# Stores on GpSimd's and SyncE's queues, states cast from those carried on, a plain copy as last step: lightning attention and an MLP on one core

## The chip, the cores and the metric

One core of a Trainium2 chip. The metric is the device time of one execution in microseconds, the median of several runs. A profile of one further execution gives the rows that are quoted.

## What is computed

Causal linear attention with a decay `lam` per head, over 4 batches, 8 heads, 768 positions and head width 64, and behind it a two-layer MLP with SiLU on the 3072 rows of 512. Cut to what matters:

```python
# attention, block of 64 positions at a time; kv_state starts at zero
intra = (qb @ kb.T * lam ** (i - j) for i >= j) @ vb
inter = (qb * lam ** (i + 1)) @ kv_state
out[:, :, sl] = intra + inter
kv_state = lam ** 64 * kv_state + (kb * lam ** (63 - i)).T @ vb
# MLP
h = x @ w_in                       # 3072 x 512 @ 512 x 2048
out = (h / (1 + exp(-h))) @ w_out  # 3072 x 2048 @ 2048 x 512
```

Inputs and output are float32; the kernel multiplies in bfloat16 and sums in float32.

## The kernel before

The sequence is cut into 12 pairs of blocks, 256 positions each, three pairs to a batch; the MLP counts in row blocks of 128. Each pair n is loaded (k, q, v, one DMA each on SyncE's queue), cast to bfloat16 (`cast`), its v scaled by the decay (`scale`, tile `vd`), and k and q are transposed: by TensorE for the first four pairs, by a DMA on SyncE's queue after them. From pair 3 on, all small TensorE products of a pair stand in one **burst** (`burst(n)`): the state of pair n (L639), the scores of pair n (L650), and the output of pair n-1 (L613, L606), on 64x64 quarters of the array. VectorE then masks the scores (`mask`, tile `st`), adds the carried state (`y`, L768), and from `y` makes two things: `xe`, the state in bfloat16 that the output products read (tiles `xs_all`, `xe_all`), and `xf`, the float32 state carried on; both are products of `y` and `lam_be` (`mult`, L394; `xe` on VectorE, `xf` mostly on GpSimd). `xt` evacuates the attention output.

The MLP's **first product** is `product1` (tag `first`, L916) with SiLU on ScalarE (`silu`, L933); its **second product** is `product2` (tag `second`, L955), evacuated by `result` and stored by `stored`. For the rows of groups 7 and 8 (row blocks 16 to 23) the first product, and for row blocks 12 to 23 the second product, are made from seven half-size products in place of eight (`product1_of_four`, L1214; `product2_of_four`, tag `seven`, L1096). They need sums of quarters: of the weights (`b`, `w`), of the inputs (`x`), and of the hidden values (`a`, tile `asum`). In groups 12 and 16 most sums `a` are made by DMA: a copy on SyncE's queue, then an accumulating DMA on GpSimd's queue (L1083). Results already summed in one PSUM bank are copied to another (`to P`, `to B`, `to R`, and `to u` in the first product), where TensorE goes on adding. Such a bank must have been filled by matmuls before; `fills` and `seeded` only assert it.

What runs when is set by `Planner`: every piece of work is a task with a key, the engines it may run on with assumed costs, its dependencies and its buffers. `order` plays the plan through once, at build time; each engine's instruction order is fixed by it, and nothing is decided on the chip. `SHIFT` moves the keys of single tasks, `HOME` fixes an engine for some. PSUM has 8 banks; a burst takes up to 7 at a time. A dummy product of `ones` (L1282) fills TensorE's gaps in the first 17 us.

At the end stand the seven products of the last four row blocks (20 to 23). The last, `m6`, is made for one row block after the other (`split`); each half is then finished by VectorE, which subtracts `o21` from the bank, and stored by ScalarE's queue:

```python
for u in range(2):
    o = Buf("rawh")
    c22 = add(at(7), {"DVE": 0.42}, lambda e, u=u, o=o: sum_of(e, osb_of(o, 1)[:, 0], part(R, u), o21.tile[:, u], AL.subtract), ...)
    stored((at(7.3)[0], 7), halves_of[1], slice(128 * us[2 + u], 128 * us[2 + u] + 128), o, c22)
```

All 25 output stores are issued by ScalarE. Line numbers are those of the kernel before; in the changed one `mult` is L411, `copy` L404 to L408, `sum_of` L1014, `stored` L961, the first product L932, the second L974 and L1123, the accumulating DMA L1110.

Of the kernel before, what the change touches and what calls it, by code (L numbers as in the profile page):

```python
# [25 lines left out]
class Buf:  # L26

    __slots__ = ("pool", "slot", "left", "tile", "pe")

    def __init__(self, pool):  # L30
        self.pool, self.slot, self.left, self.tile, self.pe = pool, None, 0, None, 0

# [5 lines left out]
def family(tag):  # L38

    return tag[:2] if isinstance(tag, tuple) and len(tag) > 2 else "none"  # L40


class Planner:
# [8 lines left out]
    SHIFT = {('a', 12, 1, 0): 11.25, ('a', 12, 2, 1): 1.25, ('a', 12, 6, 0): 4.25, ('cast', 11, 1, 1): -6.75, ('cast', 4): -10,  # L52
             ('cast', 5, 0, 1): 1.25, ('cast', 6): 5.75, ('cast', 7): 0.25, ('cast', 9, 0, 0): 3, ('cast o', 0, 0): 1.75,
             ('cast o', 0, 3): 7, ('cast o', 1, 1): 0.25, ('cast o', 2, 0): 3, ('first', 2, 2): 0.5, ('first', 2, 6): -7,
             ('first', 3): -6.5, ('first', 5, 3): -10, ('first', 5, 5): -10.75, ('first', 6, 12): 9, ('first', 6, 14): 9.5,
             ('first', 6, 8): 1.5, ('first', 7, 1, 1): -0.75, ('first', 7, 1, 2): 2.5, ('first', 7, 1, 4): 5, ('first', 7, 2, 7): 4,
             ('first', 8, 1, 1): -9.25, ('first', 8, 1, 7): 5.25, ('first', 8, 2, 1): 6, ('first', 8, 2, 2): -9.25,
             ('first', 8, 3, 1): -10.75, ('first', 8, 3, 5): 5.25, ('load w', 3, 1): -1.5, ('m3', 12): 0.5, ('mask', 5): 3,
             ('mask', 6, 1, 0): 5, ('mask', 7, 0, 0): 4, ('mask', 8, 1, 0): 1.25, ('result', 2): -6, ('result', 7): 10,
             ('scale', 11): 8.75, ('scale', 3, 0): -1, ('scale', 5, 0): -9, ('scale', 6, 0): 11.75, ('scale', 8, 0): 4,  # L60
             ('score', 1): 3, ('second', 0): -11.25, ('second', 11): 9.75, ('second', 5): 0.5, ('seven', 12): 2.25,
             ('seven', 12, 1): -0.5, ('seven', 12, 7): -6.25, ('seven', 16): 3.5, ('seven', 16, 2): 1.75, ('seven', 16, 3): -10.75,
             ('seven', 16, 4): -2.75, ('seven', 16, 6): 2.25, ('seven', 20): 3.5, ('seven', 20, 3): -1.5, ('seven', 20, 6): 0.75,
             ('seven', 20, 7): 0.5, ('silu', 3): -7.25, ('silu', 3, 4): 7, ('silu', 7): 7.75, ('silu', 8): 10, ('states', 2): 12,
             ('turn', 1): -1, ('turned', 0, 0, 1): 2.5, ('turned', 0, 1, 0): 5.5, ('turned', 1): -3.25, ('turned', 2, 0, 1): -1,
             ('w', 1): 6.5, ('w', 3): 1.25, ('x', 7): 2, ('x', 7, 3): 8.75, ('xe', 0, 0, 1): 4.5, ('xe', 3, 0, 0): 1.5,
             ('xe', 6, 0, 0): -9.5, ('xf', 9): 2.75, ('xt', 4): -2, ('xt', 8): 10.25, ('xt', 9, 1): 8.75, ('y', 10): 10,
             ('y', 11, 0, 0): -4.25, ('y', 5): 1.75}
    HOME = {('cast', 11, 1, 0): 'ACT', ('cast', 11, 1, 1): 'ACT', ('cast', 3, 0, 1): 'ACT', ('cast', 4, 0, 0): 'DVE',
            ('cast', 5, 0, 1): 'ACT', ('cast', 9, 0, 0): 'DVE', ('cast o', 0, 3): 'POOL', ('cast o', 1, 1): 'DVE',  # L70
            ('cast o', 2, 0): 'ACT', ('cast o', 2, 1): 'ACT', ('cast o', 2, 2): 'POOL', ('cast w', 1, 3): 'POOL',
            ('m3', 12): 'DVE', ('result', 2): 'DVE', ('to B', 16): 'ACT', ('to u', 8, 1): 'DVE', ('turned', 0, 0, 1): 'DVE',
            ('turned', 0, 1, 0): 'ACT', ('turned', 2, 0, 1): 'DVE', ('u3', 8, 2): 'ACT', ('w', 4, 0): 'POOL', ('w', 4, 1): 'POOL'}
# [8 lines left out]
    def add(self, key, on, fn, deps=(), bufs=(), nbytes=0, kind=None, prior=(), late=0.0, tag=None, lock=False):  # L82
        key = key if isinstance(key, tuple) else (key,)
        key = (key[0] + (self.SHIFT.get(tag, 0.0) + self.SHIFT.get(family(tag), 0.0)),) + key[1:]
        if tag in self.HOME:
            on = {self.HOME[tag]: on[self.HOME[tag]]}
        t = Task(key, on, fn, deps, list(bufs), nbytes, kind, prior, late)
        t.tag, t.lock = tag, lock
        for b in t.bufs:
            b.left += 1  # L90
            b.pe += "PE" in t.on
        self.tasks.append(t)
        return t

    def order(self):
# [11 lines left out]
        started = set()  # L107
# [58 lines left out]
        while len(out) < len(self.tasks):  # L166
# [8 lines left out]
            while release and release[0][0] <= now:  # L175
                _, _, b = heapq.heappop(release)
                self.pools[b.pool].append(b.slot)
                last[b.pool].discard(id(b))
                if not last[b.pool] and b.pool in self.becomes:
                    to, slots = self.becomes[b.pool]  # L180
                    self.pools[to] += slots
            for e in free:
# [8 lines left out]
                while ready[e]:  # L191
# [7 lines left out]
                    if any(len(self.pools[p]) < n for p, n in need.items()):  # L199
# [26 lines left out]
                for b in t.bufs:  # L226
                    if b.slot is None:
                        b.slot = self.pools[b.pool].pop(0)
# [38 lines left out]
def kernel(  # L267
# [10 lines left out]
    nc = tc.nc  # L278
# [18 lines left out]
    LOADED, MOVED, HEAD = (4, 9), (12, 16), (1.8, 1.8, 1.2, 0.6)  # L297
    TKEY, SEVENS, LAG, WSKEY, FIRST_SEVENS = 9.0, 12, 5.0, 14.0, (16, 20)
# [207 lines left out]
    def prepare(n):  # L506
# [32 lines left out]
        for g, ms in enumerate(parts):  # L539
            w = len(ms) / 4  # L540
            if n in CROSSED:
                ck.append([add((s - 1.0, g, i, c), {"DVE": 0.7 + 0.16 * c, "ACT": 1.07 + 0.17 * c}, lambda e, i=i, c=c: cross(e, i, c),
# [5 lines left out]
            cv.append(add((s - 0.8, g), {"POOL": 0.15 + 2.15 * w} if n in AWAY else {"DVE": 0.12 + 1.15 * w}, lambda e, g=g: scale_v(e, g), deps=[loads[2, g]],  # L548
# [34 lines left out]
    def burst(n, alone=False):  # L583
# [5 lines left out]
        if o:  # L589
            ob = [Buf("bank") for _ in range(2)]  # L590
# [35 lines left out]
        if new:  # L626
            kq, kqT, vd, ck, cv, turned, kq_of, t_of = ready_of[n]
            final = n % NB == NB - 1
            db, sb_ = Buf("bank"), [[Buf("bank") for _ in halves] for _ in range(2)]
# [47 lines left out]
        while rows[0] or rows[1]:  # L677
# [5 lines left out]
                max([i + 1 for i, (what, k, _, _) in enumerate(order) if what == "s" and k < 2], default=0), len(order)]  # L683
        ts, prev, spent = [], 0, -cost
# [24 lines left out]
    def attention(n):  # L709
# [41 lines left out]
        for g, ms in enumerate(parts):  # L751
# [5 lines left out]
            for c in range(len(xes)):  # L757
# [6 lines left out]
                if old:  # L764
                    src = ys[c]

                    def new_y(e, src=src, old=old, d_of=d_of, sl=sl):
# [9 lines left out]
                made[c] += [add((s + late - 0.9, 2, g), {"POOL": 0.1 + 0.6 * w} if (n, c) in XAWAY else {"DVE": 0.15 + 0.27 * w},  # L777
                                lambda e, b=b, so=so, j=j, d=d, sl=sl, x=crossed: mult(e, xe_of(b)[halves[d == halves[0]] if x else d, sl, j], so()[d],
                                                                                               rate[d, sl]),
                                deps=sd, bufs=[src, b], tag=("xe", n, g, c), lock=n >= PORT and bool(old)) for d, j in ways]  # L780
                if not final:
# [3 lines left out]
                            deps=sd, bufs=[src, f], tag=("xf", n, g, c), lock=n >= PORT and bool(old))  # L785
                    old = f, [t]
# [106 lines left out]
    full = set()  # L893

    def fills(b):

        full.add(PSUM[b.pool] + b.slot)

    def seeded(b):
        assert PSUM[b.pool] + b.slot in full  # L900

    def product1(gi):
# [6 lines left out]
        for mg in range(KO // per):  # L909
            bank, g, one = Buf("bank"), gq[mg // 4], Buf("one")  # L910
            base = us[0] - us[0] % 4 + mg * per / 4

            def mm(e, j, ko, bank=bank, mg=mg):
# [4 lines left out]
                fills(bank)  # L918
# [23 lines left out]
    def stored(key, cs, rows, osb, done):  # L942

        def store(e):
            nc.scalar.dma_start(out=out[rows, cs].rearrange("(u p) c -> p u c", p=128), in_=osb.tile)

        add(key, {"ACT": 0.1}, store, deps=[done], bufs=[osb], nbytes=(rows.stop - rows.start) * (cs.stop - cs.start) * 4e-6,
            kind=LARGE)

    def product2(u):  # L950
        gi, gp = group_of[u]
        bank, two, osb = Buf("bank"), Buf("two"), Buf("osb")

        def mm(e, ko):
            nc.tensor.matmul(psum_of(bank), lhsT=gs[gi, ko][1](1, 128 * gp, 128)[:, 0], rhs=w_out_bf[:, ko],  # L955
                             start=(ko == 0), stop=(ko == KO - 1))
            fills(bank)
# [31 lines left out]
    def duplicate(key, src, dst, deps, tag, sign=1):  # L989
        def go(e):  # L990
            seeded(dst)
# [23 lines left out]
    def sums_of_w_out():  # L1015
        for i, m in enumerate(SEVEN):
# [6 lines left out]
            def build(e, h, b=b, qs=qs, op=op):  # L1023
# [3 lines left out]
            ts = [add((TKEY + i / 4, h), {"DVE": 0.7}, lambda e, h=h, build=build: build(e, h),  # L1027
                      deps=[wload["o", 8 * r + 4 * h + ko] for r in range(2) for ko in range(4)], bufs=[b], tag=("b", m, h), lock=True,
                      prior=loaded[0])
                  for h in range(2)]  # L1030
            bsum[m] = b, [ts[ko // 4] for ko in range(8)], lambda ko, b=b: b.tile[:, ko]

    def product2_of_four(us):
        s = LAG + us[0]
        final = us[-1] == NU - 1
        A, P, B = [Buf("bank") for _ in range(3)]
        copies = {}

        R = [Buf("bank") for _ in range(2 if final else 1)]
# [9 lines left out]
        def product(i, m, bank, opens, after=(), split=False):  # L1049
# [8 lines left out]
            else:  # L1058
                for h in range(2):
# [10 lines left out]
                    if not moved:  # L1070
                        ts = add((key - 1.2, 8, h), {"DVE": 0.7}, lambda e, t=sum_tile, x=x, y=y: sum_of(e, t(), x(4), y(4), AL.subtract if m == 1 else AL.add),
# [18 lines left out]
            for p in ([(0,), (1,)] if split else [(0, 1)]):  # L1090
                for ko in range(8):
                    buf, ready, lhs = left[ko]

                    def mm(e, p=p, ko=ko, lhs=lhs):
# [3 lines left out]
                        fills(bank[0])  # L1098
# [23 lines left out]
        m5 = product(2, 5, [A], False, after=[d3, k3])  # L1122
        c12 = add(at(3), either, lambda e: copy(e, osb_of(o12), two_of(A)), deps=m5, bufs=[A, o12], tag=("c12", tag))  # L1123
        stored((at(3.3)[0], 7), halves_of[1], top, o12, c12)
        m1 = product(3, 1, [P], False, after=[d4])
        m2 = product(4, 2, [B], False, after=[d4])
# [220 lines left out]
```

## Time and profile before

| | |
|---|---|
| median of 3 runs | 205.26 us (204.59 to 206.97) |
| the profiled execution: its own time | 204.97 us |
| its span, first to last instruction | 203.1 us |
| granted TensorE clock | 1.000 |
| busy TensorE (PE), VectorE (DVE), ScalarE (ACT), GpSimd (POOL) | 196.7, 148.0, 130.5, 45.0 us |
| moved by DMA | 44.44 MB |

The profile is of one execution. A row of an engine gives the start and the length of an instruction; a wait is put down to what came last. A matmul's length is longer than the distance to the next one, since matmuls overlap; where TensorE's pace is meant, the distance of starts counts. DMA-issuing instructions of ScalarE and SyncE are not counted as busy, GpSimd's are.

### The profile page before, as it was taken

To read this page: it belongs to the slowest core of one execution; us is meant where nothing else is said; L and a number is where in the kernel's file an instruction comes from. 1 tells how busy PE (TensorE), PEld (TensorE's weight loads), DVE (VectorE), ACT (ScalarE), POOL (GpSimd) and SP (SyncE) were. 2 spreads that over 40 slices of the span, in tenths; PEclk is the share of its full clock that TensorE was granted. 3 is DMA by queue.
4 is the path that set the end of the run, shared out by engine and by line. 5 is a ranking of instruction groups with operands and counts; after the bars stand their busy time and mean duration, and the time that the engine had idled before them with its cause. 6 is when DMAs were issued, how large, how long until landed. Compare 5 with 4: busy or idle time off the path is not lost.

```text
span 203.1 us, 6063 instructions
## 1 busy us (share of the span) xinstructions
PE 196.7 (97%) x2585; PEld 144.7 (71%) x2585; DVE 148.0 (73%) x248; ACT 130.5 (64%) x199; POOL 45.0 (22%) x58
## 2 busy tenths in 40 slices
PE   7999999999999999999999999999999999999993
PEld 2677887767775557657775455558888888888882
DVE  3797859497995929569796978889585463667762
ACT  3697878568892675635887896363768696737400
POOL 4105320323100320002020045049803306000000
PEclk9999999999999999999999999999999999999999
DMA  4999999999999999999997415049995988311133
GB/s 104 329 372 383 368 360 277 367 314 375 267 259 304 247 338 302 183 307 272 307 240 223 103 58 133 28 147 233 175 125 159 219 239 151 65 52 52 61 119 135
DMA packets 71723, 44.44 MB, mean 219 GB/s; under 512 B 18448, under 2 KB 64528, under 8 KB 71696
## 3 DMA queue, kind: packets, MB, share of 16 engines
q1 hardware_dynamic: 61168, 33.56, 58.6%
q0 software_dynamic: 5376, 4.20, 14.1%
q10 hardware_dynamic: 5152, 6.30, 8.5%
q8 instruction: 20, 0.33, 0.6%
q14 instruction: 7, 0.06, 0.1%
HBM read 27.27 MB, written 6.29 MB: 165 GB/s over the span
## 4 chain that ended last, share of the span: by engine, by line
PE 89%; DMA 4%; DVE 3%; ACT 1%; issue 1%; POOL 0%
PE banks L916 25%; PE banks L955 21%; PE banks L1096 18%; PE banks L1214 12%; DMA raw_w<-in_moe_w_out_dram 4%; PE banks L1282 4%; PE banks L606 3%; PE banks L650 2%; PE banks L613 1%; DVE st L394 1%; PE banks L639 1%; PE banks L558 1%; DVE vd L394 1%; PE banks L820 1%; DVE xt L394 1%
## 5 line engine op out<-in xcount | busy, mean ns | idle before, releaser
L916 PE MATMUL banks<-xt,w_in_bf 128*128 128x256 bf16 (+1 forms) x448 | 64.6, 288 | 0.2 <-POOL w_in_bf L391 0.2
L933 ACT ACTIVATE g<-banks 128x512 bf16<-128x512 f32 x64 | 46.2, 743 | 25.3 <-PE banks L916 22.2
L916 PEld LDWEIGHTS <-w_in_bf 128*128 128x128 bf16 x448 | 43.0, 98 | 15.2 <-POOL w_in_bf L391 0.3
L955 PE MATMUL banks<-w_out_bf,g 128*128 128x512 bf16 x192 | 48.5, 379 | 0.3 <-POOL w_out_bf L391 0.3
L394 DVE TENSOR_TENSOR st<-banks,tri 128x512 bf16<-128x512 f32 (+1 forms) x42 | 30.0, 757 | 4.3 <-PE banks L650 3.6
L387 ACT ACTIVATE kq<-raw 64x512 bf16<-64x512 f32 (+3 forms) x41 | 29.7, 756 | 3.7 <-DMA raw<-in_k_dram 1.0
L955 PEld LDWEIGHTS <-g 128*128 128x128 bf16 x192 | 18.2, 98 | 18.4
L394 POOL TENSOR_TENSOR xf<-y,lam_be 128x256 f32<-128x256 f32 (+1 forms) x13 | 11.5, 888 | 65.1 <-DVE y L768 65.1
L394 DVE TENSOR_TENSOR xt<-banks,lam_xe 128x512 bf16<-128x512 f32 x24 | 16.0, 684 | 10.1 <-PE banks L606 10.1
L1096 PE MATMUL banks<-bsum,g 128*128 128x256 bf16 x160 | 21.6, 273 | 0.0
L1096 PEld LDWEIGHTS <-asum 128*128 128x128 bf16 x176 | 17.2, 98 | 2.0
L1083 POOL DMA_DIRECT2D asum<-g x8 | 13.3, 1834 | 19.0 <-PE banks L1214 11.4
L1096 PEld LDWEIGHTS <-g 128*128 128x128 bf16 x160 | 15.6, 98 | 1.9
L394 DVE TENSOR_TENSOR vd<-raw,lam_v 128x1024 bf16<-128x1024 f32 (+1 forms) x13 | 15.5, 1190 | 1.4 <-DMA raw<-in_v_dram 0.7
L1214 PE MATMUL banks<-xsum,wsum 128*128 128x256 bf16 x96 | 14.4, 273 | 0.0
L1231 ACT ACTIVATE g<-tmp 128x512 bf16<-128x512 f32 x16 | 12.1, 773 | 3.2 <-DVE tmp L997 3.0
L1083 POOL DMA_DIRECT2D g<-g x8 | 14.1, 2520 | 0.0
L1214 PEld LDWEIGHTS <-wsum 128*128 128x128 bf16 x128 | 12.4, 98 | 1.5
L1231 ACT ACTIVATE g<-banks 128x512 bf16<-128x512 f32 x16 | 11.7, 739 | 2.4 <-PE banks L1214 2.3
L1096 PE MATMUL banks<-w_out_bf,asum 128*128 128x256 bf16 x96 | 13.1, 273 | 0.0
L997 DVE TENSOR_TENSOR tmp<-banks,tmp 128x512 f32<-128x512 f32 x16 | 10.9, 685 | 2.3 <-PE banks L1214 1.3
L389 DVE CAST kq<-raw 64x1024 bf16<-64x1024 f32 (+3 forms) x17 | 9.6, 577 | 3.5 <-DMA raw<-in_k_dram 2.6
(83 smaller groups left out, 251.3 us busy)
## 6 DMA issues: line engine op xcount, KB each, us to landing
out_dram<-osb ACTq DMA_DIRECT2D x23, 256.0 KB, 2.8
raw<-in_k_dram SPq DMA_DIRECT2D x11, 512.0 KB, 6.3
raw<-in_q_dram SPq DMA_DIRECT2D x11, 512.0 KB, 6.8
raw<-in_v_dram SPq DMA_DIRECT2D x11, 512.0 KB, 6.9
raw_w<-in_moe_w_in_dram SPq DMA_DIRECT2D x8, 512.0 KB, 7.7
raw_w<-in_moe_w_out_dram SPq DMA_DIRECT2D x8, 512.0 KB, 7.5
asum<-g SPq DMA_DIRECT2D x8, 256.0 KB, 2.6
asum<-g POOLq DMA_DIRECT2D x8, 256.0 KB, 5.4
```

The lines of the kernel that those rows point to most:

```text
L387: nc.scalar.activation(o, i, AF.Copy)
L389: nc.vector.tensor_copy(o, i)
L394: (nc.vector if e == "DVE" else nc.gpsimd).tensor_tensor(o, a, b, op=AL.mult)
L916: nc.tensor.matmul(t[:, j, :], lhsT=w_in_bf[:, ko, 128 * m:128 * m + 128], rhs=xt[gi].tile[:, ko, :], start=(ko == 0), stop=(ko == KI - 1))
L933: nc.scalar.activation(t.rearrange("p j (c a r) -> p (j c) r a", c=n // U, r=2), psum_of(bank).rearrange("p (jc r a) -> p jc r a", r=2, a= ...
L955: nc.tensor.matmul(psum_of(bank), lhsT=gs[gi, ko][1](1, 128 * gp, 128)[:, 0], rhs=w_out_bf[:, ko], start=(ko == 0), stop=(ko == KO - 1))
L997: (nc.vector if e == "DVE" else nc.gpsimd).tensor_tensor(o, x, y, op=op)
L1083: nc.gpsimd.dma_start(out=x(4) if here else t(), in_=y(4), accum_op=AL.add)
L1096: nc.tensor.matmul(part(bank, u), lhsT=lhs(u), rhs=b_of(ko), stop=ko == 7, skip_group_check=True, start=opens and not ko and not u)
L1214: nc.tensor.matmul(two_of(bank)[:, f], lhsT=(wb[0].tile if wb else w_quarter(*wl))[:, ko, fs], rhs=(xsum(xr) if isinstance(xr, int) else x ...
L1231: nc.scalar.activation(t.rearrange("p j (c a r) -> p (j c) r a", c=2, r=2), src().rearrange("p (jc r a) -> p jc r a", r=2, a=64), AF.Silu)
L1282: nc.tensor.matmul((t if b.pool == "bank" else t[:, 0])[:, 0:w], lhsT=ones[:, 0:128], rhs=ones[:, 0:w], start=True, stop=True)
```

## The change

- **States.** For pairs 4 and later that carry a state on, `xe` is no longer a product of `y` and `lam_be` but a copy of `xf` with a cast, on VectorE, ScalarE or GpSimd; it waits for `xf`.
- **Stores.** `stored` can issue on three queues: row block 6 on GpSimd's, row blocks up to 11 otherwise on ScalarE's, later ones on ScalarE's or SyncE's. One store goes to GpSimd, five to SyncE, 19 stay.
- **Last step.** In the last four row blocks the products stand in another order (2, 1, 5 for 5, 1, 2), `o21` is subtracted inside the PSUM bank before the last product (`on R`), and the last two steps are plain copies, one by VectorE with its store on SyncE's queue and one by ScalarE with its store on ScalarE's.
- **Filled banks.** The planner itself now gives a copied-on sum only a bank whose last owner filled it (`fills`, `seed`).
- **Sums on GpSimd.** `b`, `a` and `x` may go to GpSimd; two sums `b`, two `x` and three `a` do, and both `w` of GpSimd return to VectorE.
- **Plan.** `SHIFT` and `HOME` have other entries, names for whole pairs, groups and fours are added, and the planner assumes 0.05 us more for a burst. TensorE's order is the same up to about 28 us and another behind that; its instructions are the same in kind and number.

```diff
-    def __init__(self, pool):
+    def __init__(self, pool, fills=False, seed=False):
...
+        self.fills, self.seed = fills, seed
...
-    SHIFT = {('a', 12, 1, 0): 11.25, ('a', 12, 2, 1): 1.25, ('a', 12, 6, 0): 4.25, ('cast', 11, 1, 1): -6.75, ('cast', 4): -10,
...
+    SHIFT = {('cast o', 2, 1): -3, ('cast o', 3, 2): 0.25, ('first', 2, 2): -1, ('first', 2, 6): -9, ('first', 3): -10.75,
...
+    HOME = {('a', 12, 1, 1): 'POOL', ('a', 20, 1, 0): 'POOL', ('a', 20, 2, 1): 'POOL', ('b', 3, 1): 'POOL', ('b', 6, 0): 'POOL',
...
+            ('to B', 16): 'ACT', ('to P', 16): 'DVE', ('to R', 16): 'DVE', ('to u', 8, 2): 'ACT', ('turned', 0, 0, 1): 'DVE',
+            ('turned', 0, 1, 0): 'ACT', ('turned', 3, 0, 1): 'DVE', ('u3', 7, 1): 'DVE', ('x', 7, 1): 'POOL', ('x', 7, 2): 'POOL',
...
             while release and release[0][0] <= now:
                 _, _, b = heapq.heappop(release)
                 self.pools[b.pool].append(b.slot)
+                (filled.add if b.fills else filled.discard)((b.pool, b.slot))
...
-                    if any(len(self.pools[p]) < n for p, n in need.items()):
+                    seeds = any(b.seed and b.slot is None and not any((b.pool, i) in filled for i in self.pools[b.pool]) for b in t.bufs)
+                    if seeds or any(len(self.pools[p]) < n for p, n in need.items()):
...
-                        b.slot = self.pools[b.pool].pop(0)
+                        slots = self.pools[b.pool]
+                        b.slot = next(i for i in slots if not b.seed or (b.pool, i) in filled)
+                        slots.remove(b.slot)
...
+    BMOVED, POOLED = (), (6,)
...
+        cost += 0.05
...
-                made[c] += [add((s + late - 0.9, 2, g), {"POOL": 0.1 + 0.6 * w} if (n, c) in XAWAY else {"DVE": 0.15 + 0.27 * w},
-                                lambda e, b=b, so=so, j=j, d=d, sl=sl, x=crossed: mult(e, xe_of(b)[halves[d == halves[0]] if x else d, sl, j], so()[d],
-                                                                                               rate[d, sl]),
+                derived = n in CROSSED and not final
+                if not derived:
...
                     t = add((s + late + (0.0 if n >= EARLY else 0.2 if n else 1.5) - 0.9, 3, g), {"POOL": 0.1 + 0.7 * w, "DVE": 0.15 + 0.27 * w} if old else {"DVE": 0.15 + 0.27 * w},
...
+                    if derived:
+                        made[c] += [add((s + late - 0.8, 2, g), {"DVE": 0.29, "ACT": 0.39, "POOL": 0.42},
+                                        lambda e, b=b, f=f, j=j, d=d, x=crossed: copy(e, xe_of(b)[halves[d == halves[0]] if x else d, :, j], f.tile[d]),
+                                        deps=[t], bufs=[f, b], tag=("xe", n, g, c), lock=True) for d, j in ways]
...
-            nc.scalar.dma_start(out=out[rows, cs].rearrange("(u p) c -> p u c", p=128), in_=osb.tile)
-
-        add(key, {"ACT": 0.1}, store, deps=[done], bufs=[osb], nbytes=(rows.stop - rows.start) * (cs.stop - cs.start) * 4e-6,
-            kind=LARGE)
+            queue = {"SP": nc.sync, "ACT": nc.scalar, "POOL": nc.gpsimd}[e]
+            queue.dma_start(out=out[rows, cs].rearrange("(u p) c -> p u c", p=128), in_=osb.tile)
+
+        u = rows.start // U
+        cost = {"SP": 0.4, "ACT": 0.36, "POOL": 1.0}
+        on = on or ("POOL" if u in POOLED else "ACT" if u < SEVENS else ("ACT", "SP"))
...
-        A, P, B = [Buf("bank") for _ in range(3)]
+        A, P, B = Buf("bank", True), Buf("bank", True, True), Buf("bank", True, True)
...
         if final:
...
+            c21, m1, c12 = second(2), first(3), fifth(4)
+
+            def begin(e, u):
+                copied(e, part(R, u), two_of(P)[:, u], -1)
+
+            d1 = [add(at(4), {"DVE": 0.42, "ACT": 0.39}, lambda e, u=u: begin(e, u), deps=m1, bufs=[P, R[u]], tag=("to R", tag, u)) for u in range(2)]
+            r1 = [add(at(4.2), {"DVE": 0.42}, lambda e, u=u: sum_of(e, part(R, u), part(R, u), o21.tile[:, u], AL.subtract),
+                      deps=[d1[u], c21], bufs=[R[u], o21], tag=("on R", tag, u)) for u in range(2)]
...
-        m6 = product(6, 6, R, False, after=d1, split=final)
+        m6 = product(6, 6, R, False, after=r1, split=final)
...
-        for u in range(2):
+        for u, on, to in ((0, {"DVE": 0.42}, "SP"), (1, {"ACT": 0.39}, "ACT")):
             o = Buf("rawh")
-            c22 = add(at(7), {"DVE": 0.42}, lambda e, u=u, o=o: sum_of(e, osb_of(o, 1)[:, 0], part(R, u), o21.tile[:, u], AL.subtract),
-                      deps=[m6[u], c21], bufs=[R[u], o21, o], tag=("c22", tag))
-            stored((at(7.3)[0], 7), halves_of[1], slice(128 * us[2 + u], 128 * us[2 + u] + 128), o, c22)
+            c22 = add(at(7), on, lambda e, u=u, o=o: copy(e, osb_of(o, 1)[:, 0], part(R, u)), deps=[m6[u]], bufs=[R[u], o], tag=("c22", tag, u))
+            stored((at(7.3)[0], 7), halves_of[1], slice(128 * us[2 + u], 128 * us[2 + u] + 128), o, c22, on=to)
```

## The prediction

> **What bounds the kernel now.** I read the page first: its busy shares, the granted clock and the chain that ended last.
>
> ```profile
> span 203.1 us, 6063 instructions
> ...
> PE 196.7 (97%) x2585; PEld 144.7 (71%) x2585; DVE 148.0 (73%) x248; ACT 130.5 (64%) x199; POOL 45.0 (22%) x58
> ...
> PEclk9999999999999999999999999999999999999999
> ...
> PE 89%; DMA 4%; DVE 3%; ACT 1%; issue 1%; POOL 0%
> ```
>
> TensorE sets the time, at full clock. The order of the changed program on TensorE has the same 2585 matmuls of the same shapes, 85 dummy ones included, and the same order up to 28 us. So the time can change only by gaps on TensorE and by the tail. Then the timeline, for the gaps. After 17.5 us I find three kinds:
>
> ```profile
> 38.61 0.60 PE L916 MATMUL banks<-xt,w_in_bf 128*128 128x256 bf16 x4
> 38.80 1.17 POOL L391 CAST w_out_bf<-raw_w 128x512 bf16<-128x512 f32 x2 [0.67 <-DMA raw_w<-in_moe_w_out_dram]
> 39.47 0.38 PE L955 MATMUL banks<-w_out_bf,g 128*128 128x512 bf16 x1 [0.26 <-POOL w_out_bf L391]
> ...
> 147.34 0.42 PE L613 MATMUL banks<-kqT,xs_all 64*64 64x128 bf16 x16
> 147.93 0.64 PE L606 MATMUL banks<-st,vd 64*64 64x128 bf16 x32 [0.17 <-PE banks L613]
> ```
>
> First, a late weight: four L916 start from 38.61, 0.109 apart, so the next matmul was due at 39.05 and came at 39.47: 0.42 us. Second, the fence inside the last burst (147.34 to 147.93), in both kernels. Third, 0.09 to 0.12 us at each change between full and quarter products, about 0.21 for a burst that stands alone. The rest runs without a gap; L1096 starts every 0.109 us up to 199.3.
>
> The tail, from the timeline and the view of tile osb:
>
> ```profile
> 199.61 0.42 DVE L997 TENSOR_TENSOR osb<-banks,osb 128x256 f32<-128x256 f32 x1 [0.45 <-PE banks L1096]
> L945 ACTq DMA_DIRECT2D out_dram<-osb x6: 351/378/379, 191.9 to 200.1; - x6
> DMA to landing us min/median/max: 1.7/2.2/2.7
> ```
>
> The last subtraction ends at 200.03, its store is issued at 200.07, lands 1.7 later, and 1.35 of closing follow.
>
> **What is saved.** *Late weight:* in the changed order 6 more L916-type matmuls stand ahead of the third second-product matmul, the one that waited: 6 x 0.109 = 0.65, more than 0.42. The loads have the same order and GpSimd's cast of that piece the same place behind the same load. Minus 0.42 (0 if the load comes 0.3 later). *Bursts:* the first burst is one piece of 64, before it was 40 and 24: minus 0.21. *Last step:* the nearest rows are ScalarE's 128x256 copy from PSUM (L985, 368 ns) for VectorE's 424, and 0.03 between the engines goes: minus 0.09; the bounds are 0 and minus 0.2. The two `on R` (2 x 0.43) come ahead of the last product and are covered by 32 matmuls of L1096, 3.5 us; behind `to R` they and the two `a` sums queued after them need 0.25 + 3 x 0.43 + 2 x 0.69 = 2.9. Uncovered they would cost 0.9.
>
> **What costs nothing, and its cover.** The stores: an issue of 0.35 to 0.38 leaves ScalarE six times, but ScalarE waits 22 us for L916 in the waits and is on 1% of the chain. SyncE's stores stand ahead of copies `asum` for row block 16, whose products come some 15 us later. GpSimd's store waits for a result; behind it stand `xf` and `xe` of pair 6, which the next burst but one needs: about 5.5 us (its result 3, an issue up to 2.5) plus 0.93 and 0.6 against 11.3 us of matmuls up to the next burst. The casts: VectorE loses products of 0.47 to 0.62, GpSimd gets ten casts of 0.31 (half of its 612 ns for 512 columns) to 0.86, one `xf` of 0.61 to 2.46 late; the chain `y`, `xf`, `xe` is 2 to 4 us, against 5.8 to 15 us of matmuls between bursts. Filled banks, the names and the 0.05 issue no instruction; a bank that must be a filled one could delay a copy, which the order doesn't show: 0 to 0.3, taken as 0.
>
> **What is added on TensorE's path.** Three places have little cover.
>
> *Burst 11* now follows directly on eight L916 of 512 columns, before it five L955 stood between. It takes seven banks. From the last start into the one bank to its release: 0.38 (the matmul) + 0.74 (L933) + 0.1; to the burst's turn five starts of 0.216 = 1.08. Plus 0.14 (0 to 0.3). Burst 12 comes 5.45 us behind burst 11, before it 10.3; VectorE needs 0.1 + 0.36 + 0.60 + 4 x 0.60 + 2 x 0.47 = 4.4 for its inputs: 0 (up to 0.4 if the `xe` are stretched).
>
> *GpSimd's line in row block 12.* Its order is a sum `x`, a DMA, a sum `x`, seven DMAs, then the sum `a` that the fifth matmul pair of product 1 reads. Before, eight DMAs stood there and nothing behind them.
>
> ```profile
> 137.56 2.32 POOL L1083 DMA_DIRECT2D g<-g  x1
> 138.30 2.88 POOL L1083 DMA_DIRECT2D asum<-g  x1
> 139.05 4.72 POOL L1083 DMA_DIRECT2D g<-g  x2
> 140.55 4.51 POOL L1083 DMA_DIRECT2D asum<-g  x1
> 141.30 5.06 POOL L1083 DMA_DIRECT2D g<-g  x1
> ...
> L997 POOL TENSOR_TENSOR wsum<-w_in_bf,wsum 128x1024 bf16<-128x1024 bf16 x2 | 4.3, 2134 | 15.9 <-DVE wsum L997 15.9
> ```
>
> They start 0.75 apart, but their ends (139.88, 141.18, 143.77, 145.06, 146.36) are 1.30 apart: 1.30 is what one occupies. Counted from the end of burst 10: `xt` is out of PSUM at 4.4 (0.2 to begin; VectorE's four masks and one `xt` 0.60 apart, as four masks take 2.47 in the timeline; three smaller pieces 0.37 apart; 0.1 for the last one's end); `x` 1.07 (half of 2134 ns) gives 5.5, or 6.2 with a blocked VectorE sum; DMA 1.45; `x` 1.07; seven times 1.30 = 9.1; the sum 2.13: ready at 19.3 to 20.0. TensorE: 5.83 + 0.23 to burst 11, 1.60 for it, 5.45, 1.25 for burst 12, 23 pairs at 0.218 = 5.0: it asks at 19.4. So a wait of 0 to 0.7; were the sum to run beside the DMAs' preparation (0.75 each) it would be 0; were it also held up by VectorE's four `x` sums (4 x 0.42), 2.3. I take 0.35. The Trainium skill (Perfetto Trace Analysis, section DMA Instruction — SWDGE (GPSIMD)) says that GpSimd's own cores write such a DMA's descriptors and that its profiled end is when the last one is written; by that the ends count and the total is the one below, by the starts it would be 0.35 less, 204.5.
>
> *The end of row block 16.* `to R`, which product 7 waits for, now stands on VectorE behind two sums `a`, while GpSimd runs two more, 2.13 each. From the end of the first products: GpSimd gets a buffer at 2.85, and if the four run one after another they end at 2.85 + 2 x 2.13 + 2 x 0.69 = 8.5; `to R` ends at 9.2, TensorE asks at 9.37. Plus 0.1 (0 to 0.3).
>
> **Sum.** Against the profiled execution, 204.97 (span 203.1 and 1.87 around it, 0.29 under the median 205.26): -0.42 - 0.21 - 0.09 + 0.14 + 0.35 + 0.10 = -0.13, so **204.8**.
>
> **Rivals.** *Only savings:* the three covers hold; 204.97 - 0.72 = 204.2. For it: no wait behind 49 us in the trace of before, where covers were as small. Against: the 1.30.
>
> *GpSimd's line becomes the bound (slower):* instructions of VectorE with only SBUF operands and GpSimd's hold each other up.
>
> ```profile
> 70.12 2.46 POOL L394 TENSOR_TENSOR xf<-y,lam_be 128x256 f32<-128x256 f32 x1 [0.81 <-DVE y L768]
> ...
> 69.96 0.68 DVE L389 CAST kq<-raw 64x1024 bf16<-64x1024 f32 x1
> 70.56 0.41 DVE L394 TENSOR_TENSOR xs_all<-y,lam_be 128x256 bf16<-128x256 f32 x1
> 70.89 1.21 DVE L394 TENSOR_TENSOR vd<-raw,lam_v 128x1024 bf16<-128x1024 f32 x1
> ```
>
> The same `xf` takes 0.61 elsewhere. With seven big sums and ten casts more on GpSimd, the sum of row block 12 comes 2.3 late and that of row block 16 0.3: 204.97 - 0.72 + 0.14 + 2.3 + 0.3 + 0.2 for burst 12 = 207.2. It decides once GpSimd's line there is over 2 us longer than worked out. Against: VectorE mostly reads PSUM there, beside which a GpSimd sum of 2.13 (117.08) kept its length. The Trainium skill (SBUF — State Buffer, section Who interferes with whom) calls it an exclusive lock, held for a whole instruction, on a VectorE instruction with two SBUF inputs among others; the row above agrees, 2.46 being about 0.61 and the two behind it. By that rule it would be this rival only if the `x` sums fall on the `a` sum.
>
> *Nothing that is on the path:* the weight is late again, the spared work was hidden: 205.0.
>
> **How the numbers follow.** Forecast 0.50, only savings 0.20, GpSimd's line 0.17, nothing 0.13. 1% (2.05 us) is about what a measurement of this kernel can tell from no change. Over 1% faster needs more than all gaps found; I leave 0.06 of the second case for it. Slower by over 1%: 0.17, and 0.03 of the forecast's upper end. Within: 0.74. The range: below, all savings and the unknown ones (-0.2, -0.3): 203.7; above, up to the third case: 207.0. The forecast's own is 204.2 to 205.8.
>
> **What would show it.** Right: TensorE without a gap near 39 us; a wait of L1123 for GpSimd's sum of row block 12, near 147 us; the last L1123 starting within 0.5 of 199.2; ScalarE's last copy of 0.37. Wrong: waits before bursts 7 to 10 on `xs_all`, or a last matmul after 201.

## The result, and the profile after

The changed kernel takes 206.83 us (median of 14 runs, 205.45 to 208.96); the kernel before, run beside it, 205.5 us (14 runs). The ratio is 1.005 with a 95% interval of 1.0028 to 1.0072: slower by half a per cent. The longest execution, 208.96, ran at a lower granted clock (0.992) and is left out of the ratio. The profiled execution took 206.17 us, 1.20 more than the profiled one of before, and its span is 204.3 us against 203.1.

From the page of the changed kernel: the span, the busy time of the engines, the granted clock and the shares of the chain that ended last.

```profile
span 204.3 us, 6084 instructions
...
PE 196.4 (96%) x2585; PEld 144.6 (71%) x2585; DVE 148.6 (73%) x237; ACT 129.3 (63%) x200; POOL 61.8 (30%) x71
...
PEclk9999999999999999999999999999999999999999
...
PE 73%; DMA 13%; SPq 5%; POOL 5%; ACT 1%; issue 1%; DVE 0%; POOLq 0%
```

The matmuls and the clock are those of before. GpSimd has 17 us more to do, and it is now 5% of the chain, with the DMAs at 13%, where the two were 0 and 4%. What TensorE waited for behind the start-up is in the view of waits (us in total, times, longest):

```profile
PE banks L1123 <- POOL asum L1014: 1.6, 1, 1.6
...
PE banks L974 <- POOL w_out_bf L408: 0.4, 1, 0.4
```

The timeline of the changed kernel shows three places and the end (start, length, engine, line, and in brackets the idle time before it with its releaser):

```profile
39.04 0.38 PE L974 MATMUL banks<-w_out_bf,g 128*128 128x512 bf16 x1
...
48.28 0.68 DVE L406 CAST kq<-raw 64x1024 bf16<-64x1024 f32 x1
48.88 1.21 DVE L411 TENSOR_TENSOR vd<-raw,lam_v 128x1024 bf16<-128x1024 f32 x1
...
48.42 2.71 POOL L408 CAST w_out_bf<-raw_w 128x512 bf16<-128x512 f32 x2 [3.48 <-DMA raw_w<-in_moe_w_out_dram]
...
50.62 1.24 PE L974 MATMUL banks<-w_out_bf,g 128*128 128x512 bf16 x5 [0.42 <-POOL w_out_bf L408]
...
133.78 1.53 POOL L1014 TENSOR_TENSOR xsum<-xt 128x512 bf16<-128x512 bf16 x1
135.99 1.33 POOL L1110 DMA_DIRECT2D asum<-g  x1 [0.68 <-DMA asum<-g]
136.87 1.64 POOL L1014 TENSOR_TENSOR xsum<-xt,xsum 128x512 bf16<-128x512 bf16 x1
137.97 1.79 POOL L1110 DMA_DIRECT2D asum<-g  x1
138.78 2.29 POOL L1110 DMA_DIRECT2D g<-g  x1
139.53 2.83 POOL L1110 DMA_DIRECT2D asum<-g  x1
143.05 1.27 POOL L1110 DMA_DIRECT2D asum<-g  x1 [0.69 <-DMA asum<-g]
143.80 4.41 POOL L1110 DMA_DIRECT2D g<-g  x3
146.08 4.28 POOL L1014 TENSOR_TENSOR asum<-g 128x1024 bf16<-128x1024 bf16 x1
...
150.41 0.39 PE L1123 MATMUL banks<-bsum,asum 128*128 128x256 bf16 x2 [1.58 <-POOL asum L1014]
...
201.27 0.38 ACT L404 ACTIVATE osb<-banks 128x256 f32<-128x256 f32 x1 [2.90 <-PE banks L1123]
```

First, the wait near 39 us is gone, as forecast. Second, a new one stands at 50.6: the first of two casts of `w_out` on GpSimd, whose load landed at 48.36, ended only at 50.57. The row holds both casts: the second took 0.61, the first 2.15, while VectorE ran a cast and a product with operands in SBUF. Third, GpSimd's line of row block 12, seven transfers and then the sum `a`. The sum ends at 150.35, and TensorE had been idle for it since 148.83 (150.41 less 1.58). Its row says 4.28 us, though the sum itself takes 2.13: the last transfer ahead ends at 148.20, and 148.20 + 2.13 is its end to 0.02.

Counted in starts of matmuls, the new holes are 1.75 and 0.58 us; the wait near 39 us gives back 0.42 and the first burst in one piece 0.21. That makes +1.70; TensorE's last matmul starts 1.67 later (200.97 against 199.30). From there to the end of the span it is 3.33 us against 3.82 before. So the span is 1.18 longer.

### The profile page after: what moved, and what is told of

It reads as the page before. It is cut to its first block, busy times and chain, and to the rows that moved or that the text cites. A ratio compares the mean times of both kernels' runs of the same rounds, so it can differ in the third digit from the quotient of the medians.

```text
span 204.3 us, 6084 instructions
## 1 busy us (share of the span) xinstructions
PE 196.4 (96%) x2585; PEld 144.6 (71%) x2585; DVE 148.6 (73%) x237; ACT 129.3 (63%) x200; POOL 61.8 (30%) x71
## 4 chain that ended last, share of the span: by engine, by line
PE 73%; DMA 13%; SPq 5%; POOL 5%; ACT 1%; issue 1%; DVE 0%; POOLq 0%
PE banks L932 22%; PE banks L974 19%; PE banks L1123 15%; PE banks L1251 10%; DMA raw_w<-in_moe_w_out_dram 6%; SPq L429 4%; DMA raw_w<-in_moe_w_in_dram 3%; DMA asum<-g 3%; POOL asum L1014 2%; PE banks L667 2%; PE banks L623 2%; POOL w_out_bf L408 1%; ACT g L948 1%; SPq L448 1%; PE banks L630 1%
## 5 line engine op out<-in xcount | busy, mean ns | idle before, releaser
L932 PE MATMUL banks<-xt,w_in_bf 128*128 128x256 bf16 (+1 forms) x448 | 66.0, 288 | 0.3 <-POOL w_in_bf L408 0.3
L404 ACT ACTIVATE kq<-raw 64x512 bf16<-64x512 f32 (+3 forms) x39 | 28.5, 762 | 3.2 <-DMA raw<-in_k_dram 1.3
L411 POOL TENSOR_TENSOR xf<-y,lam_be 128x256 f32<-128x256 f32 (+1 forms) x10 | 7.9, 792 | 42.5 <-DVE y L786 42.5
L408 POOL CAST xs_all<-xf 64x256 bf16<-64x256 f32 (+1 forms) x10 | 8.0, 798 | 35.6 <-DVE xf L411 35.2
L404 ACT ACTIVATE osb<-banks 128x512 f32<-128x512 f32 (+1 forms) x14 | 8.1, 580 | 14.9 <-PE banks L1123 7.4
L411 DVE TENSOR_TENSOR vd<-raw,lam_v 128x1024 bf16<-128x1024 f32 (+1 forms) x13 | 14.7, 1137 | 2.8 <-DMA raw<-in_v_dram 2.6
L1110 POOL DMA_DIRECT2D asum<-g x8 | 11.7, 1489 | 15.9 <-DMA asum<-g 8.5
L406 DVE CAST kq<-raw 64x512 bf16<-64x512 f32 (+3 forms) x19 | 10.4, 567 | 4.0 <-DMA raw<-in_k_dram 2.5
L1110 POOL DMA_DIRECT2D g<-g x8 | 12.5, 1915 | 0.0
```

The source lines that it names most:

```text
L404: nc.scalar.activation(o, i, AF.Copy)
L406: nc.vector.tensor_copy(o, i)
L408: nc.gpsimd.tensor_copy(o, i)
L411: (nc.vector if e == "DVE" else nc.gpsimd).tensor_tensor(o, a, b, op=AL.mult)
L932: nc.tensor.matmul(t[:, j, :], lhsT=w_in_bf[:, ko, 128 * m:128 * m + 128], rhs=xt[gi].tile[:, ko, :], start=(ko == 0), stop=(ko == KI - 1))
L1110: nc.gpsimd.dma_start(out=x(4) if here else t(), in_=y(4), accum_op=AL.add)
```

## The experiments

Each ratio is to the kernel before, run in turn with it on the same chip; it differs a little from the quotient of the two medians. The experiments were not all made on one chip, so two kernels are compared by their ratios, each known to 0.2 to 0.35%; where medians are compared, it is said. "Hole" is what lies between two starts of matmuls beyond their usual distance. Where an edit moves one task, the order written into the program stays that of the changed kernel; only the engine that executes the task is another.

**Who makes the sum of row block 12.**

```diff
-        t.fn(e)
+        t.fn({("a", 12, 1, 1): "DVE"}.get(t.tag, e))
```

> One edit to the changed kernel: the sum a for the 5th pair of product 1 in row block 12 (the one TensorE waits 1.6 us for at 148.8 us) runs on VectorE, at its place in the order, and no longer on GpSimd. If GpSimd's line sets that wait, it goes: the time falls by 1.6 to 1.8 us, to about 205.1 us beside 206.8, and TensorE's last matmul starts near 199.2 us instead of 201.0. If another dependency ends just as late (the banks of that burst, or VectorE now late with another copy), the fall is under 0.6 us.

Measured: 204.9 us, ratio 0.9971 (0.9944 to 0.9999). There is no wait for a sum; VectorE makes it in 0.69 us:

```profile
145.99 0.69 DVE L1014 TENSOR_TENSOR asum<-g 128x1024 bf16<-128x1024 bf16 x1
```

The last matmul starts at 199.33, 1.64 sooner. The hole of 1.75 and the time (1.6 us less by the ratios, 1.9 by the medians) go together, and no other dependency was hidden behind it.

**Three transfers behind the sum.** The sum stays on GpSimd; three of the seven transfers are issued later.

```diff
+    later = [x for x in planned if x[3].tag in (("a", 12, 7, 1), ("a", 12, 6, 0), ("a", 12, 6, 1))]
+    planned = [x for x in planned if x not in later]
+    n = next(i for i, x in enumerate(planned) if x[3].tag == ("a", 12, 1, 1)) + 1
+    planned[n:n] = later
```

> One edit to the changed kernel: the sum a of row block 12 stays on GpSimd, but three of the seven accumulating transfers that GpSimd writes ahead of it (those for pairs that are needed later) are issued behind it. If the transfers ahead of the sum make it late, it is ready near 148 us, before TensorE asks at 148.8, and the time falls by 1.5 to 1.8 us as if the sum were on VectorE. If the sum's own 2.1 us on GpSimd, or its buffer that comes free at 146 us, sets its end, the fall is under 0.5 us; and if the three transfers are then late for their own pairs, the wait only moves there.

Measured: 204.78 us, ratio 0.9976 (0.9954 to 0.9999), no wait for the sum. Its row in the timeline of this kernel:

```profile
146.79 2.27 POOL L1014 TENSOR_TENSOR asum<-g 128x1024 bf16<-128x1024 bf16 x1 [2.49 <-PE banks L1123]
```

It now starts when its buffer comes free (TensorE had still to read it) and takes 2.27, not 4.28. So GpSimd's slower sum does no harm here; what stood ahead of it did. This profile starts the second half of the kernel 0.9 later than that of the changed kernel, for a wait on a weight near 20 us, so its span is not used; by the ratios the time is 1.5 us less than the changed kernel's.

**The transfer with the late copy last.** Of the seven transfers behind the second sum `x`, the fourth waits for a copy on SyncE's queue. It is the fifth of the row block's eight, and is called the fifth below.

```diff
+    m = next(i for i, x in enumerate(planned) if x[3].tag == ("a", 12, 2, 1))
+    n = next(i for i, x in enumerate(planned) if x[3].tag == ("a", 12, 6, 1))
+    planned.insert(n, planned.pop(m))
```

> One edit to the changed kernel: the accumulating transfer that waits for the late copy (issued at 143.05, 0.69 after the one ahead had ended) is issued last of the seven, so that the three others fill the time in which it waits. If the late copy costs 0.65 us in GpSimd's line, the sum ends 0.65 sooner and TensorE's wait falls from 1.75 to 1.1 us. If only the number of transfers counts, the wait stays at 1.75 within 0.1.

Measured: 205.9 us, ratio 1.0045 (1.0026 to 1.0065). The ratio doesn't tell it from the changed kernel; the trace does: the seven ends are 1.30 apart without a gap, the last at 147.62, the sum ends at 149.76, and the hole is 0.89 instead of 1.75. The row of the sum in this kernel:

```profile
146.13 3.63 POOL L1014 TENSOR_TENSOR asum<-g 128x1024 bf16<-128x1024 bf16 x1
```

Of the 0.86, 0.65 is the gap that is gone; the rest is that this line began 0.2 earlier against TensorE. So the wait for the copy was worth 0.65.

**One sum `x` off GpSimd.**

```diff
-        t.fn(e)
+        t.fn({("x", 7, 2): "DVE"}.get(t.tag, e))
```

> One edit to the changed kernel: GpSimd's second sum x of row block 12 (1.64 us at 136.9, ahead of six of the seven transfers) runs on VectorE. If the copy on SyncE's queue that lands at 142.5 sets the start of the fifth transfer (143.05), the work ahead of it is worth nothing: the wait of TensorE stays 1.6 within 0.3 and the time within 0.3 us of the changed kernel's. If the sum of GpSimd's instructions sets it, all transfers move ahead by 1.1 us or more and the wait falls to 0.6 or less.

Measured: 205.51 us, ratio 1.0029 (1.0007 to 1.0052), hole 0.53. From the timeline of this kernel:

```profile
135.86 2.64 POOL L1110 DMA_DIRECT2D asum<-g  x2 [0.51 <-ACT g L948]
...
141.87 1.27 POOL L1110 DMA_DIRECT2D asum<-g  x1 [0.78 <-ACT g L1267]
142.62 4.41 POOL L1110 DMA_DIRECT2D g<-g  x3
145.90 3.28 POOL L1014 TENSOR_TENSOR asum<-g 128x1024 bf16<-128x1024 bf16 x1
```

My theory, that the landing of the late copy sets the fifth transfer whatever stands ahead, fell: that transfer starts 1.18 earlier, because the copy itself landed at 141.34 and not at 142.52. A gap of 0.78 is still there (the row names ScalarE's `g`, but the queue's own wait for the copy ended at 141.37, and it is this wait that was moved in the experiment before). In five kernels the copy landed behind the first accumulating transfer (142.27 and 142.52 in the changed kernel; 140.97 and 141.34, 141.31 and 141.58, 141.79 and 143.26, 141.72 and 141.89 in others), though issued independently of it. What ties the two, and why it is 0.2 behind in one and 1.5 in another, stays open. By the holes the work ahead and the gap both count, about 1.2 and 0.65 us. The last matmul starts 1.19 sooner too, and the median is 1.3 lower; by the ratios the time is only 0.4 lower, so how much of the hole comes back in the time is less certain here.

**The cast of `w_out` at 50 us.** The edit puts `("cast o", 2, 2)` on VectorE in the same way: alone, with the sum of row block 12 on VectorE, and with the three transfers later.

> One edit to the changed kernel: the cast of the weight tile w_out that TensorE waits 0.6 us for at 49.8 us (row block 2) runs on VectorE instead of GpSimd. If the wait comes from GpSimd's slow cast (2.71 us beside VectorE's copies), it goes and the time falls by 0.5 to 0.6 us. If VectorE's own work of that stretch is late by the cast's time in turn, or the load itself is late, the time stays within 0.2 us.

> The two edits together: the sum of row block 12 and the cast of w_out of row block 2 on VectorE. If the two waits are separate and all that the change lost, the time falls by 2.2 to 2.4 us, to about 204.5 us, 0.9 us (0.4 %) under the kernel before the change. If TensorE's lost time is made up elsewhere, or VectorE's added 1.5 us is late somewhere, the fall is 1.0 us or less.

> The changed kernel with two edits, as the fastest version so far without more work for VectorE in row block 12: the three accumulating transfers issued behind the sum, and the cast of w_out of row block 2 on VectorE. If each of the two waits is removed as in the single edits, about 204.4 us (204.8 with the first alone, 0.3 to 0.4 less for the cast), 0.4 to 0.5 % under the kernel before. If one brings back the other, 204.8 or more.

Measured: 206.05 us, ratio 1.001 (0.9974 to 1.0045) alone; 204.59 us, 0.9964 (0.994 to 0.9989) with the sum; 204.25 us, 0.9969 (0.9951 to 0.9987) with the transfers later. From the timeline of the last:

```profile
50.21 0.43 DVE L406 CAST w_out_bf<-raw_w 128x512 bf16<-128x512 f32 x1 [1.03 <-DMA raw_w<-in_moe_w_out_dram]
...
50.69 1.24 PE L974 MATMUL banks<-w_out_bf,g 128*128 128x512 bf16 x5 [0.48 <-DVE w_out_bf L406]
```

The cast now takes 0.43, but starts at 50.21, when the load has landed, and TensorE waits as long as before. In these traces the piece landed at 50.25, 49.13 and 50.19, in the changed kernel's at 48.36; the view of waits has 0.2 at this place for the first, none for the second, and for the third 0.5 with another 0.4 for the next piece. In the first two the holes, 0.41 and 0.20, end right behind ScalarE's cast of the other half of the piece (51.97 and 50.76), which stands behind two casts `kq` on ScalarE. So the slow cast is what ended the wait in the changed kernel's profile, but the load and ScalarE's cast stand close behind it. By the ratios the time is 0.1 to 0.8 lower with the edit (by the medians 0.3 to 0.8), which the intervals don't tell from nothing: the gain of this edit alone is inconclusive. The two combinations have the lowest ratios of the study, 0.3 to 0.4% under the kernel before, but aren't told from the same kernels without this edit (0.9971 and 0.9976).

**The states as products again.** Where the source of a state is `y`, VectorE multiplies as before; in the same order, and once with the two edits above.

```diff
-    lambda e, ...: copy(e, xe_of(b)[...], f.tile[d]),
+    lambda e, ...: mult("DVE", xe_of(b)[...], so()[d], rate[d]) if src.pool == "y" else copy("DVE", xe_of(b)[...], f.tile[d]),
```

> One edit to the changed kernel: the states for the output are again products on VectorE of the new row block with its rates, not casts from the states carried on. If these states are off the path that sets the end, the time stays within 0.2 us of the changed kernel's. If the casts hold up the first product of a row block, it falls by more than 0.3 us; if VectorE's added products make it late, it rises by more than 0.3 us.

> The changed kernel with the sum of row block 12 and the cast of w_out on VectorE (204.6 us) and the states for the output as products on VectorE again. If the 1.3 us that TensorE waited for xt near 139 us with these products come from VectorE's line and were only hidden by the later wait for the sum, they stay: 205.8 us, 1.2 more, with no wait for a sum. If the wait belonged to the pile-up of sums on GpSimd and VectorE, it goes and the time is 204.6 to 204.8.

Measured: 206.12 us, ratio 1.0037 (1.0012 to 1.0062), and 205.73 us, ratio 1.0028 (1.0004 to 1.0051). From the waits and VectorE's timeline of the first:

```profile
PE banks L1251 <- DVE xt L411: 1.3, 1, 1.3
```

```profile
134.99 1.64 DVE L1014 TENSOR_TENSOR asum<-g 128x1024 bf16<-128x1024 bf16 x1
136.56 2.27 DVE L1014 TENSOR_TENSOR xsum<-xt 128x512 bf16<-128x512 bf16 x1
138.75 0.68 DVE L411 TENSOR_TENSOR xt<-banks,lam_xe 128x512 bf16<-128x512 f32 x1
```

And the same three rows with the casts, from the timeline of the changed kernel:

```profile
133.62 0.68 DVE L1014 TENSOR_TENSOR asum<-g 128x1024 bf16<-128x1024 bf16 x1
134.22 1.38 DVE L1014 TENSOR_TENSOR xsum<-xt 128x512 bf16<-128x512 bf16 x1
136.65 0.69 DVE L411 TENSOR_TENSOR xt<-banks,lam_xe 128x512 bf16<-128x512 f32 x1 [1.05 <-PE banks L623]
```

With the products VectorE comes 1.4 late to its two sums and both fall beside GpSimd's sums `x`, so 2.06 us become 3.91 (with the casts they fall beside the first of them only), and VectorE is done with them 3.2 late. Of this, 1.05 is VectorE's idle time ahead of `xt`, so `xt` ends 2.1 late; with the casts it had ended 0.67 ahead of the matmul that reads it (137.34 and 138.01), and what is left is a hole of 1.44 at 137.9. In the first kernel that hole only took the place of the wait for the sum of row block 12, which was then ready; the time hardly tells. In the second, where that wait is gone, the hole stands alone: the time is 1.3 us above that of the kernel without the products by the ratios, 1.1 by the medians (205.73 against 204.59), where 1.2 was expected. So in this order the casts are worth 1.1 to 1.3 us, against my expectation that they are worth nothing; it holds for this order alone.

**The closing.** Three kernels: the changed one with the store of row block 6 on ScalarE's queue; the kernel before with that store on GpSimd's; the kernel before with the new last step alone.

```diff
-        t.fn(e)
+        t.fn({("store", 6, 0): "ACT"}.get(t.tag, e))
```

```diff
-            nc.scalar.dma_start(out=out[rows, cs]...)
+            (nc.gpsimd if rows.start == 6 * U else nc.scalar).dma_start(out=out[rows, cs]...)
```

```diff
+            c21, m1, c12 = second(2), first(3), fifth(4)
...
+            r1 = [add(at(4.2), {"DVE": 0.42}, lambda e, u=u: sum_of(e, part(R, u), part(R, u), o21.tile[:, u], AL.subtract), ...)]
...
-        m6 = product(6, 6, R, False, after=d1, split=final)
+        m6 = product(6, 6, R, False, after=r1, split=final)
```

> One edit to the changed kernel: the store of row block 6 is issued on ScalarE's queue again, not on GpSimd's. If the closing after the last store is 0.4 us shorter only because one transfer fewer runs on the hardware queues (which moves the last store to the semaphore that SyncE's closing waits come to last), the tail from the last matmul's start to the span's end is 3.8 us again, not 3.4, and the time 0.4 us longer. If the shorter tail comes from the last step's plain copy or the queues of the last stores, the tail stays 3.4 us.

> One edit to the kernel before the change: the store of row block 6 is issued on GpSimd's queue. If the closing depends on which semaphore the last hardware transfer falls on, the tail from the last matmul's start to the span's end goes from 3.8 to 3.4 us and the time falls by 0.4 us, to about 205.1. If not, both stay within 0.1 us.

> The kernel before the change with only the new last step of a row block in two halves: the order of its products, the sum of bank and product moved ahead, the last copies as plain copies, the last half's stores on the queues of SyncE and ScalarE. By the theory of the semaphores the tail shortens by no more than 0.05 us (the last copy 0.38 instead of 0.43) and the time stays within 0.2 us of before. By the rival, that the last step is what shortened the tail, the tail is 3.4 us and the time 0.4 us lower.

| kernel | ratio (interval) | last matmul's start to the span's end |
|---|---|---|
| before | 1 | 3.82 us |
| changed | 1.005 (1.0028 to 1.0072) | 3.33 |
| changed, store 6 on ScalarE | 1.0088 (1.0058 to 1.0119) | 3.76 |
| before, store 6 on GpSimd | 0.9979 (0.9954 to 1.0005) | 3.37 |
| before, new last step | 0.9999 (0.9967 to 1.0031) | 3.76 |

The ratio of the fourth is as forecast, though its interval just holds 1; the ends in the profiles tell it without doubt. The new last step shortens the end by 0.04 to 0.06; moving one early store to GpSimd's queue shortens it by 0.43 to 0.45, in both kernels. The trace's event records say why. At the end SyncE waits for eight semaphores in a fixed order, 0.06 us apart; the transfers of SyncE's and ScalarE's queues take these eight in turn:

```
before:  last store on semaphore 100, landed 201.77
SyncE waits: 100 at 201.79, 102, 104, 105, 107, 108, 109, 110 at 202.22; span ends 203.12
changed: last store on semaphore 110, landed 203.39
SyncE waits: 100 at 201.31, 102, 104, 105, 107, ... 109 at 202.80, 110 at 203.41; span ends 204.29
```

Before, the last store had the first semaphore in that order, and the seven others were gone through behind it; one transfer fewer on those queues moves it to the last, and the seven are done before it lands.

## Why the prediction was wrong, step by step

The forecast was 204.8, a shade faster; the kernel is slower, 206.83, 2.0 above it. Both the forecast and the rivals were worked out from the profiled execution of before; the like figure of the changed kernel is 206.17, 1.4 above the forecast and 1.0 under the rival of GpSimd's line, 207.2. That the median comes near this rival is luck: the line was 1.0 to 1.7 us longer than worked out, not over 2, VectorE's stretching of the first sum `x` cost nothing, and the rival's waits at row block 16 and burst 12 didn't come. Added up with the sizes measured, the terms are -0.42 - 0.21 - 0.05 + 1.75 + 0.58 - 0.43 = +1.22; the span is 1.18 longer. Of the signs named ahead, the missing gap near 39 us, the wait for the sum of row block 12 and ScalarE's last copy (0.38) came; the last start within 0.5 of 199.2 did not (200.97).

- *Late weight, -0.42, and bursts, -0.21:* right, both rows as forecast.
- *Last step, -0.09:* 0.04 to 0.06.
- *Burst 11, +0.14, and the end of row block 16, +0.10:* nothing; TensorE shows no wait at either.
- *GpSimd's line in row block 12, +0.35:* this is the step that failed, by its size: bounded at 0 to 0.7 and taken as 0.35, it measured 1.75. The place, the moment at which TensorE asks (19.4 us behind burst 10, measured 19.4) and the 1.30 for each transfer were right; the sum came at 21.0, not at 19.3 to 20.0. I had summed the line as work alone, one instruction behind the other. Two of its transfers also wait for copies: the first begins 0.68 after the sum `x` ahead of it, when a copy has landed at 135.40, and the fifth 0.69 after the transfer ahead. Against the upper end, 0.44 is lost up to the end of the second `x`, and 0.59 over the seven transfers, which is the gap less what they are shorter than 1.30. VectorE did stretch the first `x` (1.53 for 1.07), but that ended at 135.31, ahead of the copy, and cost nothing. So a term that was taken in the middle of its bounds needed its releasers, not only its durations.
- *"The loads have the same order and GpSimd's cast of that piece the same place", and no term for other casts:* the cover was worked out for the wait of before only. The next piece but one then had a GpSimd cast of 2.15 beside VectorE and left a hole of 0.58, for which the sum had no term; by how much the time would fall without it stays open, as the experiment on this cast shows. The profile before had shown such a stretch (`xf`, 2.46 for 0.61). The Trainium skill (SBUF — State Buffer, section Who interferes with whom) says that a VectorE cast in a fast mode, or an instruction of it with two SBUF inputs, and GpSimd keep each other out for a whole instruction, and that whichever issues first decides who waits. The rows agree in which engine waited: GpSimd's cast ends 0.48 behind VectorE's `vd` (48.88 + 1.21 = 50.09), a little less than the 0.61 that it takes alone, and in the kernel with products it was VectorE's sums that were stretched, 2.06 to 3.91.
- *The closing:* -0.43, for which there was no term. I counted the moved store as costing nothing and saw no gain in it.
- *The casts of the states, no cost:* right as to cost; that VectorE's spared time is what keeps `xt` of row block 12 in time in this order, 1.1 to 1.3 us, wasn't seen.

Which reading of GpSimd's DMAs holds, starts or ends, is settled: the sum ended 2.13 to 2.16 behind the *end* of the last transfer ahead in three kernels (148.20, 147.62, 147.03). The Trainium skill's statement that the end of such a row is when GpSimd's cores have written the last descriptor (Perfetto Trace Analysis, section DMA Instruction — SWDGE (GPSIMD)) agrees.

## What to carry to other kernels

When a result is moved behind a line of transfers on a slow queue, add to the line's work, transfer by transfer, what each one waits for; a gap in the middle of a line that is otherwise tight goes in full into the end. Where a busy engine has to issue, put what is needed first ahead: here the order of three transfers was worth 1.5 us by the ratios, as much as a faster engine for the sum (1.6). And undo one edit at a time before a change is judged: one misplaced sum hid that the rest of it was a gain of about 0.3%, most of it perhaps the closing (0.2% on the kernel before, with an interval that just holds 1).

## What the runs showed of the hardware that was not expected

- Which semaphore the last store falls on decides 0.43 to 0.45 us of the end: SyncE's closing waits cost 0.06 each and run in a fixed order.
- A transfer on GpSimd's queue starts 0.53 to 0.59 us after the copy that it waits for has landed (135.40 and 135.99, 142.52 and 143.05; 135.48 and 136.07 in another kernel).
- The row of a GpSimd sum that stands behind such transfers begins before it can run: 4.28, 3.63 and 3.28 us for the same sum, which takes 2.27 where no transfer is under way ahead of it.
- Of the four copies of 256 KB on SyncE's queue for row block 12, three landed 2.5 to 3.3 us after their issue; the fourth took 4.5 to 5.8 in five kernels, and landed 0.2 to 1.5 behind the first accumulating transfer of GpSimd's queue.
